# Two of the first block's three up-projection sets as eight plain products, with those on the first heads ahead of the last heads

## Chip, cores, metric

One core of one Trainium2 chip. The metric is the device time of one execution in microseconds; lower is better. Kernels of one batch ran on the same chip beside the kernel before.

## The reference

Linformer attention, then an MLP mixer over tokens and channels:

```python
# batch 8, heads 8, seq 1024, head_dim 64, k_proj 64; d_model 512, d_tok 256, d_ch 1536
k_proj = einsum('ks,bhsd->bhkd', E, k);  v_proj = einsum('ks,bhsd->bhkd', F, v)
attn   = softmax(scale * q @ k_proj^T) @ v_proj
x  = heads side by side                                # (8, 1024, 512)
h  = relu(x^T @ w_tok1) @ w_tok2                       # token mixing
u  = x + h^T
h2 = relu(u @ w_ch1) @ w_ch2                           # "up", then "down"
out = u + h2
```

A block is half a batch: 512 rows of u, 16 blocks in all. Each block has three up-projection sets (`m` = 0, 1, 2).

## The kernel before

Up and down projections use Winograd's variant of Strassen's scheme: seven half-size products in place of eight, paid for with sums on VectorE: sums S of the activations, combinations of the weights (made once, partly in place), and relu-adds on the way out.

```python
def combine(T, b11, b12, b21, b22, cols, name, n, reads):
    def one(k, out, in0, in1, *deps):
        dve(cols, lambda: nc.vector.tensor_sub(out=out, in0=in0, in1=in1), ps=False,
            reads=reads + [(name, n, i) for i in deps], writes=[(name, n, k)])
    one(7, T[1], b22, b12)
    one(5, b12, b12, b11, 7)        # writes over the raw weights b12
    one(6, T[0], b22, b12, 5)
    one(4, T[2], b21, T[0], 6)

def up_set(j, m):                   # seven products of 4 matmuls, 256 columns each
    ...
    product(1)
    act(512, ... copy(view("y"), view("x")) ...)
    product(2);  relu(0, "x")
    product(6);  keep(ub, "ub")
    product(7)
    product(5);  keep(ua, "ua")
    dve(512, ... add_relu(G[:, 2, cs], view("z"), ua) ...)
    product(3);  relu(1, "y")
    product(4)
    dve(512, ... add_relu(G[:, 5, cs], view("z"), ub) ...)
    ... # four totals on VectorE for the down projection
```

The kernel doesn't issue these in the order of the text. Each call of `pe`, `dve`, `act` and so on adds a job with an estimated duration and a priority. A planner then plays the program through when it is built, with a queue for each engine and eight PSUM banks, and takes the job that can start first; among jobs within 0.02 us it takes the one with the lowest priority number:

```python
while any(can.values()):
    pick = None
    for e, js in can.items():
        ...
        t0 = min(c[0] for c in cands) + 0.02
        c = min((c for c in cands if c[0] <= t0), key=lambda c: (c[1], c[2]))
        if pick is None or c[0] < pick[0]:
            pick = c
    ...
return sorted(order, key=lambda j: j.at)
```

What comes out is fixed: each engine runs its instructions in this order.

The softmax here doesn't subtract the row's maximum and nothing guards it: scores larger than these inputs give would overflow.

Of the kernel before, what the change touches and what calls it, by code (L numbers as in the profile page):

```python
# [11 lines left out]
ALU = mybir.AluOpType  # L12
ACT = mybir.ActivationFunctionType
EARLY = 12.0
WHOLE = 3
TWO = 2
SUMS = 60.0
# [181 lines left out]
def kernel(  # L199
# [13 lines left out]
    nc = tc.nc  # L213
    P = 128
# [18 lines left out]
    SETS = CC // 4  # L233
# [20 lines left out]
    def tile_of(shape, dtype, name):  # L254
        return sb.tile(shape, dtype, tag=name, name=name)
# [4 lines left out]
    def bank(b):  # L260

        return banks[b.at] if b.span == 1 else psum[:, b.at : b.at + 2]
# [11 lines left out]
    wc1_sb = tile_of([P, 2, 2, 2, DC // 2], BF16, "wc1_sb")  # L274
# [22 lines left out]
    G_t = [tile_of([P, 7, C2, 2 * P], BF16, f"G{i}") for i in range(2)]  # L297
# [25 lines left out]
    def pe(n, cols, fn, **kw):  # L323
        t = n * MM[cols]
        return pl.add("PE", t, t, fn, **kw)

    def dve(cols, fn, ps=True, **kw):
        t = cols / 960 + 0.07 if ps else cols / 1920 + 0.07
        return pl.add("DVE", t, t + 0.09, fn, **kw)

    def act(cols, fn, **kw):
        t = cols / 1200 + 0.07
        return pl.add("ACT", t, t + 0.105, fn, **kw)
# [40 lines left out]
    for m in range(SETS):  # L374
        cs = slice(m * cw, (m + 1) * cw)
        for ch in range(2):
# [5 lines left out]
                writes=[("w1", m, ch)], prio=next(first),  # L382
            )
    w2_v = moe_w_ch2.rearrange("(ch cc p) d -> p ch cc d", ch=2, p=P)
    for c in range(0, C2, 3):
        for ch in range(2):
            ld(
                0.786, dma(wc2_sb[:, ch, c : c + 3], w2_v[:, ch, c : c + 3]),
                writes=[("w2", ch, c // 3)], prio=next(first),
# [6 lines left out]
    def due_u(s, n):  # L396
        return 8.2 * s + U_AT[n]
# [43 lines left out]
    def combine(T, b11, b12, b21, b22, cols, name, n, reads):  # L441
        def one(k, out, in0, in1, *deps):
            dve(
                cols, lambda: nc.vector.tensor_sub(out=out, in0=in0, in1=in1), ps=False,
                reads=reads + [(name, n, i) for i in deps], writes=[(name, n, k)],
            )

        one(7, T[1], b22, b12)
        one(5, b12, b12, b11, 7)
        one(6, T[0], b22, b12, 5)  # L450
        one(4, T[2], b21, T[0], 6)

    for m in range(SETS):
        cs = slice(m * cw, (m + 1) * cw)
        combine(
            [wT1[:, n, :, cs] for n in range(3)],
            *(wc1_sb[:, dh, :, ch, cs] for dh in range(2) for ch in range(2)),
            cols=2 * cw, name="W1", n=m, reads=[("w1", m, 0), ("w1", m, 1)],
        )
    for c in range(2):  # L460
        cs = slice(3 * c, 3 * c + 3)
        combine(
            [wT2[:, n, cs] for n in range(3)],
            *(wc2_sb[:, ch, cs, dh * DH : (dh + 1) * DH] for ch in range(2) for dh in range(2)),
            cols=3 * DH, name="W2", n=c, reads=[("w2", 0, c), ("w2", 1, c)],
        )
# [46 lines left out]
    def k_transpose_dma():  # L513
        sp(
            2.5,
            lambda: nc.sync.dma_start_transpose(
                out=kT.rearrange("p h c k -> p h (c k)"), in_=kb.rearrange("p h r d -> p (h r d)")
            ),
            reads=[("kb", i, h) for i in range(2) for h in range(H)],
            writes=[("kT", i, h) for i in range(2) for h in range(H)], prio=None,  # L520
        )
# [248 lines left out]
    def quarter(j, sh, dh):  # L770
        return uT_t[j % 2][:, 2 * sh : 2 * sh + 2, 2 * dh : 2 * dh + 2, :]
# [330 lines left out]
    def w1_of(n, dd, c):  # L1102
        cs = slice(c * P, (c + 1) * P)
        if n in (1, 2, 3, 5):
            dh, ch = {1: (0, 0), 2: (1, 0), 3: (1, 1), 5: (0, 1)}[n]
            return wc1_sb[:, dh, dd, ch, cs]
        return wT1[:, {6: 0, 7: 1, 4: 2}[n], dd, cs]
# [7 lines left out]
    def a_of(j, n, dd):  # L1115
        if n in (1, 2, 4):
            sh, dh = {1: (0, 0), 2: (0, 1), 4: (1, 1)}[n]
            return uT_t[j % 2][:, 2 * sh : 2 * sh + 2, 2 * dh + dd, :]
        return S_t[j % 2][:, {5: 0, 6: 1, 7: 2, 3: 3}[n], :, dd, :]
# [4 lines left out]
    def add_relu(out, in0, in1):  # L1124
        nc.vector._custom_dve(TENSOR_ADD_SAT, out=out, in0=in0, in1=in1, s0=FMAX, s1=0.0)  # L1125

    def up_set(j, m):
        s = SETS * j + m
        G = G_t[j % 2]
        cs = slice(2 * m, 2 * m + 2)  # L1130
        bk = {n: Bank("U", seeded=n == "y") for n in "xyz"}
        ub, ua = ub_t[s % 2], ua_t[s % 2]

        def view(n):
            return bank(bk[n]).rearrange("p (c s) -> p c s", c=2)

        def g(n):
            return ("G", j % 2, n, m)

        def mm(n):  # L1140
            t = view(X_OF[n])
            for c in range(2):
                for dd in range(2):
                    nc.tensor.matmul(  # L1144
                        t[:, c, :], w1_of(n, dd, 2 * m + c), a_of(j, n, dd),
                        start=(n in (1, 7) and c == 0 and dd == 0), stop=(c == 1 and dd == 1),
                        skip_group_check=True,
                    )

        def product(n):  # L1150
            src = [("S", j % 2, {5: 0, 6: 1, 7: 2, 3: 3}[n])] if n in (5, 6, 7, 3) else [
                ("uT", j % 2, i) for i in ((0, 1) if n == 1 else (2, 3))
            ]
            src += [("W1", m, n)] if n in (5, 6, 7, 4) else [("w1", m, 0 if n < 3 else 1)]
            first = n in (1, 7)
            b = bk[X_OF[n]]
            pe(
                4, 256, lambda: mm(n), reads=src, takes=[b] if first else [],
                uses=[] if first else [b], prio=due_u(s, n),
                after=[g(i) for i in {1: (0,), 7: (2, 3, 4, 5, 6)}.get(n, ())],  # L1160
            )

        def relu(n, src):
            act(
                512,
                lambda: nc.scalar.activation(out=G[:, n, cs], in_=view(src), func=ACT.Relu),  # L1166
                writes=[g(n)], uses=[bk[src]],
            )

        def keep(dst, name):  # L1170
            act(
                512, lambda: nc.scalar.copy(out=dst, in_=view("y")), writes=[(name, s % 2)],  # L1172
                uses=[bk["y"]],
            )

        def total(n, a, b, add):
            f = nc.vector.tensor_add if add else nc.vector.tensor_sub
            c = slice(2 * both[0], 2 * both[-1] + 2)
            dve(
                512 * len(both), lambda: f(out=G[:, n, c], in0=G[:, a, c], in1=G[:, b, c]), ps=False,  # L1180
                reads=[("G", j % 2, i, mm) for i in (a, b) for mm in both],
                writes=[("G", j % 2, n, mm) for mm in both],
            )

        product(1)
        act(
            512, lambda: nc.scalar.copy(out=view("y"), in_=view("x")), takes=[bk["y"]],  # L1187
            uses=[bk["x"]], after=[g(1)],
        )
        product(2)  # L1190
        relu(0, "x")
        product(6)
        keep(ub, "ub")
        product(7)
        product(5)
        keep(ua, "ua")
        dve(
            512, lambda: add_relu(G[:, 2, cs], view("z"), ua), reads=[("ua", s % 2)],
            writes=[g(2)], uses=[bk["z"]],
        )  # L1200
        product(3)
        relu(1, "y")
        product(4)

        dve(
            512, lambda: add_relu(G[:, 5, cs], view("z"), ub), reads=[("ub", s % 2)],
            writes=[g(5)], uses=[bk["z"]],
        )
        both = TOTALS[m] if SINGLE <= j < NSB - 1 else (m,)
        if both:  # L1210
            total(3, 5, 2, True)
            total(5, 0, 5, False)
            total(4, 3, 0, False)
            total(6, 1, 4, False)

    out_v = out.rearrange("b (p si) d -> b p si d", p=P)

# [191 lines left out]
    def front(b, begin, end):  # L1409
        units = []  # L1410

        def unit(cost, f):
            units.append((cost, f))

        hn = H // 2 if b == 1 else H
        for i in range(H // hn):
# [3 lines left out]
            else:  # L1420
                unit(1.9, lambda t: kv_proj(b, 0, H, t - EARLY, True))
                unit(0.0, lambda t: k_transpose_dma())
# [7 lines left out]
        for h in range(H):  # L1430
            if h + 2 < H:
                unit(0.4, lambda t, h=h: scores(h + 2, t))
            if b >= WHOLE:
                unit(0.5, lambda t, h=h: attend_whole(h, t))
# [46 lines left out]
    for j in plan:  # L1481
# [7 lines left out]
        n = len(nc.cur_bb.bb.instructions)  # L1489
# [37 lines left out]
```

## Time and profile before

| | kernel before |
|---|---|
| time, 3 runs | 423.50 us (422.79 to 423.52) |
| PE busy | 98% of the span |
| VectorE busy | 83%; 100% from 30 to 50 us |
| chain that ended last | PE 91%, VectorE 4%, ScalarE 2%, DMA 1% |

PE (the matrix engine) is the bound. A "hole" below is time between two matmuls beyond their normal spacing (0.109 us at 256 columns). A row of the profile gives 0.27 us for such a matmul, so the rows overlap and short holes do not show in the busy share. The lines, and how they are read, are in the prediction.

### The profile page before, as it was taken

Reading aid. Unit: us, or ns where it says so; the run is one execution under the profiler, and the core shown is the slowest. Engines: PE = TensorE matmul, PEld = TensorE weight load, DVE = VectorE, ACT = ScalarE, POOL = GpSimd, SP = SyncE. Lnnn points to the kernel's source line nnn. Section 1 sums busy time; section 2 is a strip of 40 time slices with the busy share of each in tenths; the row PEclk is TensorE's granted clock in tenths of the full one; section 3 lists DMA queues with packets and bytes.
Section 4 is the critical chain, followed back from the end, with each engine's and each line's share of the span. In section 5 each row is a group of like instructions: output and inputs, shape, how many; then the busy total and the mean of one; then the engine's idle time right before and its main releaser. Section 6 shows DMA issues by size and latency. Waiting matters only on the chain.

```text
span 421.2 us, 9421 instructions
## 1 busy us (share of the span) xinstructions
PE 412.1 (98%) x3838; PEld 347.7 (83%) x3838; DVE 348.0 (83%) x747; ACT 231.8 (55%) x444; POOL 66.2 (16%) x104
## 2 busy tenths in 40 slices
PE   7999999999999999999999999999999999999996
PEld 3587877688788888888798888888898899988885
DVE  2359969679679798988889899898988798997685
ACT  1858884475636546564645556655646645354530
POOL 8453220022003030022103020212100000010110
PEclk9999999999999999999999999999999999999999
DMA  9999999996975989398974989999760501250223
GB/s 166 207 201 206 207 206 164 225 177 140 216 145 103 195 133 235 64 186 141 207 163 94 191 139 224 163 200 179 153 146 0 152 27 76 50 151 2 102 100 103
DMA packets 96668, 62.48 MB, mean 148 GB/s; under 512 B 62064, under 2 KB 92272, under 8 KB 96624
## 3 DMA queue, kind: packets, MB, share of 16 engines
q0 software_dynamic: 34944, 45.09, 54.5%
q1 hardware_dynamic: 61056, 16.00, 21.6%
q10 hardware_dynamic: 624, 0.79, 0.7%
q8 instruction: 30, 0.49, 0.5%
q14 instruction: 14, 0.11, 0.1%
HBM read 59.24 MB, written 16.78 MB: 180 GB/s over the span
## 4 chain that ended last, share of the span: by engine, by line
PE 91%; DVE 4%; ACT 2%; DMA 1%; issue 0%; DVEq 0%
PE psum L1253 34%; PE psum L1144 33%; PE psum L848 4%; PE psum L484 4%; PE psum L597 3%; PE psum L964 3%; PE psum L656 2%; DMA o<-in_F_dram 1%; PE psum L620 1%; DVE u L1071 1%; PE psum L736 1%; PE psum L687 1%; PE psum L581 1%; PE psum L405 1%; PE psum L711 1%; PE psum L1032 1%
## 5 line engine op out<-in xcount | busy, mean ns | idle before, releaser
L1253 PEld LDWEIGHTS <-G 128*128 128x128 bf16 x1344 | 130.6, 98 | 19.7 <-issue 1.5
L1253 PE MATMUL psum<-wc_sb,G 128*128 128x256 bf16 x768 | 102.5, 273 | 0.5 <-ACT psum L1309 0.2
L1166 ACT ACTIVATE G<-psum 128x512 bf16<-128x512 f32 x96 | 57.3, 600 | 56.0 <-PE psum L1144 55.4
L1144 PEld LDWEIGHTS <-wc_sb 128*128 128x128 bf16 x768 | 73.8, 98 | 10.9 <-issue 0.6
L1253 PE MATMUL psum<-wT,G 128*128 128x256 bf16 x576 | 77.7, 273 | 0.1
L1180 DVE TENSOR_TENSOR G<-G 128x512 bf16<-128x512 bf16 (+1 forms) x140 | 69.5, 516 | 1.0
L1144 PEld LDWEIGHTS <-wT 128*128 128x128 bf16 x576 | 55.7, 98 | 9.0 <-issue 1.2
L1144 PE MATMUL psum<-uT,wc_sb 128*128 128x256 bf16 x384 | 57.7, 273 | 0.2 <-ACT psum L1187 0.2
L1144 PE MATMUL psum<-S,wc_sb 128*128 128x256 bf16 x384 | 57.6, 273 | 0.1
L1144 PE MATMUL psum<-S,wT 128*128 128x256 bf16 x384 | 55.6, 273 | 0.4 <-DVE S L781 0.4
L1287 POOL DMA_DIRECT2D out_dram<-o x30 | 16.4, 548 | 240.2 <-DVE o L1293 125.6
L1125 DVE CUSTOM_DVE_ANT_0 G<-psum,ub 128x512 bf16<-128x512 f32 x48 | 32.9, 685 | 15.3 <-PE psum L1144 15.1
L1172 ACT COPY ua<-psum 128x512 f32<-128x512 f32 x48 | 28.2, 588 | 30.1 <-PE psum L1144 29.7
L606 ACT ACTIVATE a<-psum 128x512 bf16<-128x512 f32 x64 | 36.4, 602 | 12.4 <-PE psum L597 11.8
L1293 DVE TENSOR_TENSOR o<-psum,u 128x512 f32<-128x512 f32 x55 | 37.5, 683 | 6.4 <-PE psum L1253 6.3
L1187 ACT COPY psum<-psum 128x512 f32<-128x512 f32 x48 | 27.8, 580 | 18.9 <-DVE G L1125 9.9
L1125 DVE CUSTOM_DVE_ANT_0 G<-psum,ua 128x512 bf16<-128x512 f32 x48 | 32.7, 682 | 5.0 <-ACT ua L1172 4.6
L1172 ACT COPY ub<-psum 128x512 f32<-128x512 f32 x48 | 28.2, 588 | 7.0 <-PE psum L1144 6.3
L1144 PE MATMUL psum<-uT,wT 128*128 128x256 bf16 x192 | 28.8, 273 | 0.1
L673 DVE TENSOR_TENSOR x_sb<-psum,rdn 128x512 bf16<-128x512 f32 x40 | 27.4, 686 | 0.6
L597 PE MATMUL psum<-qT,kT 128*128 128x512 bf16 x64 | 21.5, 380 | 0.6 <-ACT kT L549 0.6
L346 POOL DMA_DIRECT2D v_sb<-in_v_dram x18 | 13.5, 749 | 50.7 <-DMA uT<-u 48.0
(108 smaller groups left out, 547.2 us busy)
## 6 DMA issues: line engine op xcount, KB each, us to landing
out_dram<-o POOLq DMA_DIRECT2D x30, 512.0 KB, 4.2
k_sb<-in_k_dram POOLq DMA_DIRECT2D x14, 512.0 KB, 8.5
v_sb<-in_v_dram POOLq DMA_DIRECT2D x14, 512.0 KB, 10.3
q_sb<-in_q_dram POOLq DMA_DIRECT2D x14, 512.0 KB, 9.9
wc_sb<-in_moe_w_ch_dram POOLq DMA_DIRECT2D x6, 256.0 KB, 12.3
wc_sb<-in_moe_w_ch_dram POOLq DMA_DIRECT2D x4, 384.0 KB, 12.3
k_sb<-in_k_dram POOLq DMA_DIRECT2D x4, 256.0 KB, 6.8
v_sb<-in_v_dram POOLq DMA_DIRECT2D x4, 256.0 KB, 7.3
```

What stands on the lines that cost most here:

```text
L484: nc.tensor.matmul(t[0:KP, 0:hn], ET_sb[:, si, :], k_sb[:, hs, si, :], start=a, stop=z)
L597: lambda: nc.tensor.matmul(bank(bk), kT[:, h].rearrange("p c k -> p (c k)"), qT[:, h].rearrange("p j s -> p (j s)"), start=True, stop=True,),
L606: lambda: nc.scalar.activation(out=a_t[h // 2 % 2][:, h % 2], in_=bank(bk), func=ACT.Exp, scale=scale),
L673: lambda: nc.vector.tensor_tensor(out=x_sb[:, :, h * D : (h + 1) * D].rearrange("p (n c) d -> p n c d", n=2), in0=view()[:, :, :, 0:D], in ...
L1125: nc.vector._custom_dve(TENSOR_ADD_SAT, out=out, in0=in0, in1=in1, s0=FMAX, s1=0.0)
L1144: nc.tensor.matmul(t[:, c, :], w1_of(n, dd, 2 * m + c), a_of(j, n, dd), start=(n in (1, 7) and c == 0 and dd == 0), stop=(c == 1 and dd == 1),
L1166: lambda: nc.scalar.activation(out=G[:, n, cs], in_=view(src), func=ACT.Relu),
L1172: 512, lambda: nc.scalar.copy(out=dst, in_=view("y")), writes=[(name, s % 2)],
L1180: 512 * len(both), lambda: f(out=G[:, n, c], in0=G[:, a, c], in1=G[:, b, c]), ps=False,
L1187: 512, lambda: nc.scalar.copy(out=view("y"), in_=view("x")), takes=[bk["y"]],
L1253: nc.tensor.matmul(to, G[:, G_OF[n], cc, t * P : (t + 1) * P], w2_of(n, cc), start=(n in opens and (t == 0 or alone) and cc == 0), stop=(c ...
L1293: 512, lambda: nc.vector.tensor_add(out=dst, in0=view(src), in1=u_of(sh, dh)),
```

## The change

The intent: before the first product with an S operand, PE waits for VectorE. Plain products need neither S nor combined weights, and those on the first half of the model dimension need only heads 0 to 3. So PE can work while the last heads are finished, at the price of eight groups in place of seven.

```diff
+PLAIN = (0, 1)
@@ combine
+                after=reads if k == 5 else [],
@@
-    for m in range(SETS):
+    def combine_w1(m):
         ...
+    for m in range(SETS):
+        if m not in PLAIN:
+            combine_w1(m)
@@
+    def up_plain(m):
+        ...
+        bk = {(sh, ch): Bank("U") for sh in range(2) for ch in range(2)}
+        quarters = [(0, 0), (0, 1), (1, 1), (1, 0)]
+        for dh in range(2):                       # first heads, then last heads
+            for n, q in enumerate(quarters):
+                pe(
+                    4, 256, lambda q=q, dh=dh: mm(q, dh),
+                    reads=[("uT", 0, 2 * dh + hp) for hp in range(2)] + [("w1", m, q[1])],
+                    takes=[bk[q]] if dh == 0 else [], uses=[bk[q]] if dh else [],
+                    prio=due_u(m, 1) - 1.0 + dh + 0.1 * n,
+                )
+        for q, to in zip(quarters, (0, 1, 2, 5)):
+            act(512, lambda q=q, to=to: nc.scalar.activation(out=G[:, to, cs], in_=view(q), func=ACT.Relu), ...)
+        combine_w1(m)
@@ up_set
+        if j == 0 and m in PLAIN:
+            up_plain(m)
+            both = (m,)
+            totals()
+            return
```

More of the change, by code (lines that the diff above doesn't have):

```diff
@@ L1125, in add_relu, with view, mm @@
         nc.vector._custom_dve(TENSOR_ADD_SAT, out=out, in0=in0, in1=in1, s0=FMAX, s1=0.0)
+    def up_plain(m):
+        G = G_t[0]
+        cs = slice(2 * m, 2 * m + 2)
+        bk = {(sh, ch): Bank("U") for sh in range(2) for ch in range(2)}
+        def view(q):
+            return bank(bk[q]).rearrange("p (c s) -> p c s", c=2)
+        def mm(q, dh):
+            sh, ch = q
+            for c in range(2):
+                for dd in range(2):
+                    nc.tensor.matmul(
+                        view(q)[:, c, :],
+                        wc1_sb[:, dh, dd, ch, (2 * m + c) * P : (2 * m + c + 1) * P],
+                        quarter(0, sh, dh)[:, :, dd, :],
+                        start=(dh == 0 and c == 0 and dd == 0), stop=(c == 1 and dd == 1),
+                        skip_group_check=True,
+                    )
[7 more added lines that the diff above has]
+                    prio=due_u(m, 1) - 1.0 + dh + 0.1 * n,
+                )
+        for q, to in zip(quarters, (0, 1, 2, 5)):
+            act(
+                512,
+                lambda q=q, to=to: nc.scalar.activation(out=G[:, to, cs], in_=view(q), func=ACT.Relu),
+                writes=[("G", 0, to, m)], uses=[bk[q]],
+            )
+        combine_w1(m)
     def up_set(j, m):
@@ L1130, in up_set @@
         cs = slice(2 * m, 2 * m + 2)
-        bk = {n: Bank("U", seeded=n == "y") for n in "xyz"}
+        plain = j == 0 and m in PLAIN
+        bk = {} if plain else {n: Bank("U", seeded=n == "y") for n in "xyz"}
         ub, ua = ub_t[s % 2], ua_t[s % 2]
@@ L1183, in total, with totals @@
             )
+        def totals():
+            total(3, 5, 2, True)
+            total(5, 0, 5, False)
+            total(4, 3, 0, False)
+            total(6, 1, 4, False)
+        if j == 0 and m in PLAIN:
[3 more added lines that the diff above has]
+            return
         product(1)
@@ L1210, in up_set @@
         if both:
-            total(3, 5, 2, True)
-            total(5, 0, 5, False)
-            total(4, 3, 0, False)
-            total(6, 1, 4, False)
+            totals()
     out_v = out.rearrange("b (p si) d -> b p si d", p=P)
```

## The prediction

> **What bounds the kernel now.** I began with the busy shares and the chain that ended last (two parts of the page), then cut the first 100 us into windows, and read the waits, the chain and the timeline only where a window fell short.
>
> ```profile
> PE 412.1 (98%) x3838; PEld 347.7 (83%) x3838; DVE 348.0 (83%) x747; ACT 231.8 (55%) x444; POOL 66.2 (16%) x104
> PE 91%; DVE 4%; ACT 2%; DMA 1%; issue 0%; DVEq 0%
> ```
>
> PE is busy for 98% of the span, and 91% of the chain is PE. The end is set by the time when PE starts to run without a break, plus the PE work that is left then. A saving on another engine counts only where PE waits for it.
>
> PE's own waits are few, and nearly all lie near the start:
>
> ```profile
> PE psum L1085 <- DVE u L1071: 0.5, 1, 0.5
> PE psum L1144 <- DVE S L781: 0.4, 1, 0.4
> ```
>
> In the chain in order of time (start, length, what) the same place is the only long stretch after 28 us that isn't PE:
>
> ```profile
> 28.96 0.40 DVE x_sb L637 x2
> 29.35 0.24 issue
> 29.59 1.28 DVE u L1071 x2
> 30.87 0.33 DVE wT L444
> 31.21 0.60 DVE u L1071
> 31.81 0.33 DVE wc_sb L444
> 32.14 1.20 DVE u L1071 x2
> 33.34 0.15 DVE wT L444
> 33.48 0.10 issue
> 33.59 1.28 DVE u L1071 x2
> 34.87 0.33 DVE wT L444
> 35.20 0.68 DVE S L781 x2
> 35.88 0.04 issue
> 35.93 2.40 PE psum L1144 x20
> ```
>
> From the last attention heads (x_sb) to the first product with an S operand at 35.93 us, VectorE works through residual adds (L1071), the weight combinations of Winograd's scheme for the first set (L444), and the S sums (L781). From 35.93 us on PE runs products. The windows (PE, PEld, DVE, ACT, POOL, clock, DMA share, GB/s) agree:
>
> ```profile
> 30.97:35.93 4.96, 4.06 (x56) 3.48 (x54) 4.96 (x12) 4.66 (x10) 2.90 (x4) 1.00 1.34 203
> 35.93:47.00 11.07, 10.96 (x99) 9.57 (x99) 11.07 (x28) 9.01 (x18) 1.48 (x2) 1.00 1.24 207
> ```
>
> VectorE is full in both; PE has holes only in the first. After 100 us the 20 us windows show 19.7 to 20.0 us of PE, up to the tail. So what the change can win lies almost wholly before 36 us.
>
> **What the skill says, and whether the trace agrees.** (1) "TensorE: Matmul & The Clock Gate", section Back-to-back issue gap, gives a warm matmul of N columns N/2.4 + 2.5 ns, so 109 ns at 256. The timeline agrees: groups of four 256-column products start 0.43 to 0.44 us apart (41.09, 41.52, 41.96), though the rows give 273 ns for one. The row includes the pipeline, so I count 0.109 us and not 0.273. The same page also gives lower sustained figures for other sizes; the trace decides. (2) "VectorE: DVE Perf Modes", section The perf-mode tier table, has tensor_tensor in bf16 from SBUF at twice the rate of one with a PSUM operand. Here the bf16 combination of 512 columns takes 0.33 us and the residual add from PSUM 0.60 to 0.64 us of VectorE (starts in the timeline). It agrees. (3) "Perfetto Trace Analysis", section Identifying the Most-Contended Engine, says matmul busy time is no measure of nearness to the roofline. It applies here: 4.06 us "busy" of 4.96 hides more idle time than 0.9 us, as worked out below.
>
> **The change part by part.**
>
> *Added on PE.* Each of the two sets has eight groups of four matmuls in place of seven: one group more per set, 2 x 4 x 0.109 = **+0.87 us**, and on a full engine it is on the path. Moving data have 256 columns as before, so there is no other cost.
>
> *Filled on PE.* How idle is PE between 30.97 and 35.93 us? The timeline lists 28 transposes (0.056 us apart), 16 matmuls of token mixing with 128 columns (0.058 us) and two groups of products (0.44 us): 1.57 + 0.93 + 0.87 = 3.4 us of work in 4.96, so 1.6 us idle. (Between 28.4 and 30.97 there is no idle time by the same count.) The four plain groups on the first half of the model dimension need only the transposed heads 0 to 3 and the first set's weights. The weights are there in time: PoolE issues the 24th load when a wc_sb load has landed, at 29.3 us, and the next two at 30.9 and 32.2 us; counted down the order of loads, set 0 is complete at about 29 us and set 1 at about 32 us. The transposed heads are copied by ScalarE from 31.45 us, and today's first product starts at 32.33. So plain products can start at 32.0 to 32.3 us: 4 groups of set 0, and one of set 1, since the pool of up-projection banks holds five. That is 5 x 0.44 = 2.2 us of work for a hole of about 1.4 us after 32 us: enough to close it. **-1.3 us**, with 0.1 left for a bank or a late copy.
>
> *Removed from VectorE ahead of the first products.* The four combinations of set 0 (4 x 0.33 = 1.3 us) leave the stretch 30.8 to 35.1, and the plain products do not wait for the S sums. The residual adds of the last heads can then come earlier; that makes sure that the second half of the products (from about 34.3 us) follows without a hole. The time is already in the 1.3 us and isn't counted twice.
>
> *Removed later.* A set loses two relu-adds on VectorE (2 x 0.60 us) and goes from five to four operations on ScalarE. So 2.4 us of VectorE and some 1.1 us of ScalarE fall away between 36 and 55 us. VectorE is full there, but PE scarcely waits: the chain has one place, 38.35 to 40.22, of which PE's timeline shows about 0.27 us of true idle time (the previous group ends near 39.95). This place is in set 0 and goes: **-0.25 us**. The other relief is off the path.
>
> *Moved.* The combinations of sets 0 and 1 come after the plain products that read the raw weights, 8 x 0.33 = 2.7 us, due before the second block's first set. Set 2 and that block's sums come between; from about 34 us VectorE has some 8 us for 4 x 0.33 (set 2's combination) + 8 x 0.33 (two blocks' sums) + 1.2 (set 2's relu-adds) + 4 x 0.33 (set 0's combination) = 6.5 us. It fits, with not much to spare.
>
> Sum: +0.87 - 1.3 - 0.25 = **-0.7 us**, from 423.5 to **422.8 us**.
>
> **The rivals.** (a) *Nothing is won, extra work is paid*: the plain products get no banks while the token-mixing outputs wait in PSUM for VectorE, or take PE ahead of the last heads, whose token mixing and transposes then come late. ScalarE's four copies from 31.45 to 35.3 us, without pause, speak for it: they don't get faster. Then the hole stays and +0.87 is paid: about 424.3 us. Against it: VectorE frees the banks up to 1.3 us sooner. (b) *The combination becomes the new wait*: it writes over weights that plain products read, so it can't run before these end, near 40 us for set 1; VectorE stays at 100% for 15 us. If the second block's first set waits for 1 us, 423.8 us. Against it: the 8 us for 6.5 above, and the planner puts the next batch's attention between. (c) *The static order shifts as a whole.* The order of instructions is planned from estimated durations, and one early change moves banks and priorities everywhere. The present plan has few holes later (0.3 us each at 160 to 180 and 220 to 240 us, some at 80 to 100 and the tail), so there is less to win than to lose: -0.7 to +1 us. (d) *A larger gain*: VectorE's 2.4 us do count, because its queue falls behind the plan by less, and the later holes go as well: about 421.3 us.
>
> **Range and chances.** The arithmetic gives -0.7; its parts alone span about -1.2 (all holes filled) to +0.9 (none). The reshuffled order adds about 1 us either way, and three runs of the kernel before span 0.7 us. That makes 420.8 to 424.4 for 8 in 10. Two per cent is 8.5 us, more than all the PE idle time after the first 10 us, and five times any loss above: faster by over 2% 0.01, within 2% 0.98, slower by over 2% 0.01.
>
> **What would show it right or wrong.** Right: PE starts plain products (a new line, on uT and wc_sb) near 32 us; the waits of PE for VectorE's u and S between 30 and 36 us are gone; PE's work between 32 and 36 us grows by 1.2 us or more; there are 8 more matmuls, and PE's total busy time is about the same while the span is 0.5 to 1 us shorter. Wrong: plain products that start after 34 us, or a wait of PE for L444 or for S between 40 and 45 us (rival b); PE idle time that shows up after 100 us (rival c); or PE work up to 36 us unchanged while the total grows by 0.9 us (rival a).

## The result

| | before | changed |
|---|---|---|
| time, 4 runs each | 423.51 us (422.79 to 424.21) | 424.69 us (424.22 to 425.45) |
| ratio, 95% interval | | 1.003 (1.0005 to 1.0054) |
| span of the profiled run | 421.2 us | 422.3 us |

A ratio here is the mean time of one kernel's fast runs over the mean of the other's fast runs of the same rounds, so it is not quite the ratio of the medians that are quoted.

The kernel got slower by 0.3%: 424.69 us, where 422.8 was forecast with a range up to 424.4. Yet the start went largely as foreseen. First the busy shares and the chain, from the page of the changed kernel:

```profile
PE 413.4 (98%) x3846; PEld 348.4 (83%) x3846; DVE 345.9 (82%) x743; ACT 230.6 (55%) x442; POOL 66.1 (16%) x104
PE 78%; DVE 13%; DMA 4%; ACT 2%; issue 1%; POOL 1%; DVEq 0%; POOLq 0%; ACTq 0%
```

There are eight more matmuls, as foreseen. VectorE's share of the chain went from 4% to 13%, although VectorE has less to do than before (345.9 us, was 348.0). The windows at the start (the same columns as in the prediction):

```profile
30.97:35.93 4.96, 4.71 (x64) 4.37 (x62) 4.48 (x11) 3.21 (x7) 3.00 (x4) 1.00 1.34 203
35.93:47.00 11.07, 10.99 (x104) 9.71 (x102) 11.07 (x31) 9.09 (x18) 1.48 (x2) 1.00 1.24 206
```

From 30.97 to 35.93 us PE now has 4.71 us busy in place of 4.06. The timeline of PE (start, length, line) shows what fills it:

```profile
32.26 0.39 PE L1092 MATMUL psum<-ident,u 128*128 128x128 bf16 x4
32.49 1.91 PE L1147 MATMUL psum<-uT,wc_sb 128*128 128x256 bf16 x16
34.23 0.83 PE L1092 MATMUL psum<-ident,u 128*128 128x128 bf16 x12
35.29 0.66 PE L1066 MATMUL psum<-hT_sb,wt_sb 128*128 128x128 bf16 x8 [0.23 <-ACT uT L1098]
35.79 3.66 PE L1147 MATMUL psum<-uT,wc_sb 128*128 128x256 bf16 x32
```

The plain products are line L1147. Four groups start at 32.49 us, eight follow from 35.79 and the last four at 39.50. There is one short wait, for ScalarE's copy of a transpose. Counted by the spacing of matmuls, PE was idle for 1.39 us between 32 and 36 us in the kernel before and is idle for 0.46 in this one, and the hole of 0.27 us at 39.95 is gone. A new one of 0.23 us stands at 42.57, where a product waits for a ScalarE copy (L1244). It is too short for the list of waits. In the waits of PE over the whole span, those for VectorE's u and S near 35 us are gone:

```profile
PE psum L1307 <- ACT psum L1363: 0.4, 1, 0.4
...
PE psum L1190 <- DVE S L788: 0.3, 1, 0.3
...
PE psum L1066 <- ACT uT L1098: 0.2, 1, 0.2
```

The wait for S that is listed is another one, at 373 us. Where did the time go, then? Late windows, first of the kernel before:

```profile
280.00:340.00 60.00, 60.00 (x561) 52.33 (x559) 52.23 (x108) 33.99 (x64) 4.98 (x8) 1.00 0.56 120
340.00:400.00 60.00, 60.00 (x555) 54.00 (x553) 49.97 (x96) 28.69 (x54) 3.19 (x6) 1.00 0.23 71
```

and of the changed kernel:

```profile
280.00:340.00 60.00, 59.86 (x557) 51.73 (x555) 52.49 (x111) 33.78 (x64) 4.95 (x8) 1.00 0.78 143
340.00:400.00 60.00, 59.66 (x550) 53.55 (x548) 51.12 (x97) 28.98 (x54) 3.20 (x6) 1.00 0.23 71
```

After 280 us, with the change long past, PE gets through 4 and 5 matmuls less in the same time. By the spacing of matmuls its idle time from 280 to 400 us is 1.37 us, and 0.31 in the kernel before. One such place, in the chain in order of time of the changed kernel:

```profile
363.98 0.68 DVE G L1132
364.66 0.60 DVE u L1001
365.26 0.60 DVE a L1001
365.86 0.60 DVE o L1347
...
372.44 0.60 DVE G L1132
373.04 0.68 DVE S L788 x2
373.72 0.04 issue
373.76 0.60 PE psum L1190 x4
```

VectorE works for 10 us on end, and PE waits for the S sums behind it (a hole of 0.42 us). The profile of the kernel before has only PE in its chain there.

**A ledger of PE's idle time.** To put numbers to it I took every matmul of the timeline, gave it its spacing (0.109 us at 256 columns, 0.216 at 512, 0.056 at 128; the projections of k and v, which run side by side (their starts are 0.01 us apart), once a pair), and subtracted the sum from the time passed. This needs a profile with all its matmul records; the five of the table have them. The clock is started 1.2 us after VectorE's first residual add, because the add itself starts at a time that hangs on the landing of the loads (26.9 to 28.3 us in these five), for which a kernel isn't to blame: one load of the token weights is issued at 8.72 or 8.73 us in all fourteen profiles, and lands between 19.8 and 21.1. The last three rows belong to experiments below.

| profile | idle to +23 us | idle from +23 to +380 us | work over before | sum against before | span less start of first add |
|---|---|---|---|---|---|
| before | 2.57 | 3.92 | 0 | 0 | 394.04 |
| changed | 1.37 | 5.23 | 0.87 | +0.98 | 395.00 |
| after_order_from_52 | 1.15 | 4.46 | 0.87 | -0.01 | 393.84 |
| one_set_order_from_56 | 1.43 | 4.46 | 0.44 | -0.16 | 393.74 |
| one_set_order_from_180 | 1.42 | 3.81 | 0.44 | -0.82 | 393.26 |

The changed kernel won 1.20 us of idle time in the first 23 us, paid 0.87 us of work, and was then 0.3 us ahead, about half of what was predicted. Over the next 357 us it collected 1.31 us more of idle time than the kernel before. The last column, which doesn't depend on the count, agrees to 0.2 us.

A sixth profile, that of `one_set_own_order` (below), has all its records too, and closes as well. Counted once more with slightly different spacings, it has 1.23 us less idle time than the kernel before at the start, 2.92 us more later and 0.44 us more work, +2.13 us in all. Its last column is 396.17, also +2.13.

Two cautions. The row of the changed kernel is one profile, of an execution of 424.22 us, its fastest; a second profile of the same kernel (`after_again`) has 396.21 in the last column. And the granted clock in the first 20 us was 0.90 and 0.93 in the changed kernel's profile and 1.00 in the other. The ledger starts behind this: from 20 us on both have 1.00.

### The profile page after: what moved, and what is told of

It reads as the page before. It is cut to its first block, busy times and chain, and to the rows that moved or that the text cites. A ratio compares the mean times of both kernels' runs of the same rounds, so it can differ in the third digit from the quotient of the medians.

```text
span 422.3 us, 9433 instructions
## 1 busy us (share of the span) xinstructions
PE 413.4 (98%) x3846; PEld 348.4 (83%) x3846; DVE 345.9 (82%) x743; ACT 230.6 (55%) x442; POOL 66.1 (16%) x104
## 4 chain that ended last, share of the span: by engine, by line
PE 78%; DVE 13%; DMA 4%; ACT 2%; issue 1%; POOL 1%; DVEq 0%; POOLq 0%; ACTq 0%
PE psum L1307 30%; PE psum L1190 28%; PE psum L855 4%; DMA q_sb<-in_q_dram 3%; PE psum L491 3%; PE psum L971 2%; DVE G L1226 2%; PE psum L604 2%; DVE G L1132 2%; PE psum L663 2%; DMA v_sb<-in_v_dram 2%; DVE u L1007 1%; DVE a L1001 1%; PE psum L1147 1%; DVE o L1347 1%
## 5 line engine op out<-in xcount | busy, mean ns | idle before, releaser
L1212 ACT ACTIVATE G<-psum 128x512 bf16<-128x512 f32 x92 | 54.6, 598 | 59.9 <-PE psum L1190 59.5
L1190 PEld LDWEIGHTS <-wc_sb 128*128 128x128 bf16 x736 | 70.8, 98 | 11.4 <-issue 0.4
L1190 PEld LDWEIGHTS <-wT 128*128 128x128 bf16 x552 | 53.4, 98 | 8.0 <-issue 0.9
L1190 PE MATMUL psum<-uT,wc_sb 128*128 128x256 bf16 x368 | 55.2, 273 | 0.1
L1190 PE MATMUL psum<-S,wc_sb 128*128 128x256 bf16 x368 | 55.1, 273 | 0.0
L1190 PE MATMUL psum<-S,wT 128*128 128x256 bf16 x368 | 53.3, 273 | 0.3 <-DVE S L788 0.3
L1244 ACT COPY psum<-psum 128x512 f32<-128x512 f32 x46 | 26.5, 576 | 23.9 <-PE psum L1190 9.9
L1132 DVE CUSTOM_DVE_ANT_0 G<-psum,ub 128x512 bf16<-128x512 f32 x46 | 31.5, 685 | 9.3 <-PE psum L1190 9.2
L1132 DVE CUSTOM_DVE_ANT_0 G<-psum,ua 128x512 bf16<-128x512 f32 x46 | 31.4, 682 | 8.6 <-ACT ua L1218 8.5
L1218 ACT COPY ub<-psum 128x512 f32<-128x512 f32 x46 | 27.0, 587 | 4.8 <-PE psum L1190 4.0
```

The source lines that it names most:

```text
L1132: nc.vector._custom_dve(TENSOR_ADD_SAT, out=out, in0=in0, in1=in1, s0=FMAX, s1=0.0)
L1190: nc.tensor.matmul(t[:, c, :], w1_of(n, dd, 2 * m + c), a_of(j, n, dd), start=(n in (1, 7) and c == 0 and dd == 0), stop=(c == 1 and dd == 1),
L1212: lambda: nc.scalar.activation(out=G[:, n, cs], in_=view(src), func=ACT.Relu),
L1218: 512, lambda: nc.scalar.copy(out=dst, in_=view("y")), writes=[(name, s % 2)],
L1244: 512, lambda: nc.scalar.copy(out=view("y"), in_=view("x")), takes=[bk["y"]],
```

## The experiments

Theory A: the change does what it should, and the time is lost later, because the planner, given other jobs at the start, orders the whole rest differently, and the new order has more holes. Theory B ("rival B" in the expectations): the change itself costs (extra products, combinations made late, banks), whatever the order.

| label | median us | range us | ratio to before, 95% interval |
|---|---|---|---|
| after_again | 425.04 | 424.22 to 425.48 | 1.0032 (1.001 to 1.0053) |
| after_late_as_before | 424.03 | 423.06 to 424.75 | 1.001 (0.9989 to 1.0031) |
| after_best_order | 425.12 | 422.85 to 425.86 | 1.0031 (1.0006 to 1.0057) |
| before_best_order | 424.84 | 423.36 to 426.62 | 1.003 (1.0003 to 1.0058) |
| before_shaken_1 | 424.62 | 424.48 to 426.98 | 1.0042 (1.0015 to 1.0068) |
| before_shaken_2 | 427.58 | 427.41 to 428.43 | 1.01 (1.008 to 1.012) |
| before_late_as_after | 424.87 | 424.69 to 425.12 | 1.0031 (1.0011 to 1.0051) |
| before_two_more_groups | 424.60 | 423.96 to 425.27 | 1.0025 (1.0005 to 1.0044) |
| after_order_from_52 | 423.36 | 423.10 to 424.11 | 0.999 (0.9974 to 1.0006) |
| one_set_order_from_56 | 422.95 | 422.89 to 423.31 | 0.9985 (0.9971 to 0.9998) |
| one_set_order_from_180 | 422.32 | 422.05 to 422.54 | 0.9967 (0.9954 to 0.9981) |
| one_set_own_order | 425.32 | 425.13 to 426.17 | 1.0041 (1.0026 to 1.0056) |

The kernel before had a median of 423.41 (11 runs) beside the first four, 423.51 (12 runs, those eleven among them) beside the next four, and 423.64 (9 runs) beside the last four. All twelve kernels gave right results.

### The changed kernel again

No edit. It ran on the same chip as the next seven; the last four ran on another.

> The changed kernel once more, to have it on the same chip as the next three. Both theories: 1.0 to 1.5 us (0.3%) slower than the kernel before.

425.04 us: the loss is there again. Its profile shows something else: laid beside the first profile of the same kernel, VectorE's instructions are 0.05 us apart at 57 us, but 0.27 at 107, 0.34 from 110, 0.90 at 126, and that to the end. PE's timeline of the second profile shows two waits that the first doesn't have:

```profile
107.21 0.61 PE L1190 MATMUL psum<-uT,wc_sb 128*128 128x256 bf16 x4 [0.17 <-DMA uT<-u]
125.67 0.39 PE L604 MATMUL psum<-qT,kT 128*128 128x512 bf16 x1 [0.38 <-DMA kT<-kb]
```

Both are for transposing DMAs that SyncE issues. The first took 6.60 us from issue to landing, 5.95 in the first profile, and landed at 107.16 in place of 106.82. The other landed at 125.62 in place of 124.28, as it was issued 2.3 us later. By the spacing of matmuls these two waits are holes of 0.31 and 0.54 us. So this order leaves PE open to the landing of DMAs, which differs between runs of one kernel.

### The changed start, the old order later

The planner gets a list of jobs, `LATE`: those that the kernel before starts after 150 us of planned time, in its order. An engine takes them in just this order, after all its other jobs.

```diff
+LATE = [968, 799, 1171, 830, 636, ...]
+        # lines: each engine's late jobs in order; soon: how many other jobs it has left
+        def may(j):
+            if j.n not in is_late:
+                return True
+            return not soon[j.eng] and lines[j.eng][0] == j.n
@@ the choice of candidates
+                    if not may(j):
+                        continue
@@ once a job is chosen
+            if j.n in is_late:
+                lines[j.eng].pop(0)
+            else:
+                soon[j.eng] -= 1
```

> The changed kernel, in which every engine takes the jobs that the kernel before begins after 150 us of planned time in exactly the order in which the kernel before has them. The plain products and all that precedes stay. Theory A (the start of the change works, 1.25 us of PE idle time filled for 0.87 us of extra products, and the time is lost after 100 us through small holes of another static order): the later holes go, 423.2 to 423.9 us, level with the kernel before and 1 us under the changed kernel; PE's idle time from 150 us to the end as in the kernel before. Rival B (the change itself costs: the extra products, the late weight combinations or the banks slow what follows, whatever the order): stays at 424.5 to 425 us.

424.03 us, 0.1 above the stated band, but 1.0 us less than the changed kernel. The trace makes it sharper. Two instructions of ScalarE's timeline in the kernel before, far apart:

```profile
158.22 0.58 ACT L506 CAST kb<-psum 64x512 bf16<-64x512 f32 x1 [1.39 <-PE psum L487]
...
409.13 0.57 ACT L1309 COPY psum<-psum 128x512 f32<-128x512 f32 x1 [1.85 <-DVE G L1180]
```

and the same two in this kernel:

```profile
158.65 0.58 ACT L600 CAST kb<-psum 64x512 bf16<-64x512 f32 x1 [1.39 <-PE psum L581]
...
409.56 0.57 ACT L1450 COPY psum<-psum 128x512 f32<-128x512 f32 x1 [1.85 <-DVE G L1313]
```

Both are 0.43 us later, and so is every ScalarE instruction sampled between (0.42 or 0.43), down to the same idle time before it. From where the order is the same, the two kernels run the same in these two profiles. So nothing of the change reaches past that point except a fixed distance: theory B can't be right about the stages after it.

### The old start, the changed order later

The mirror image: the kernel before, with the jobs that the changed kernel starts after 100 us of planned time in the changed kernel's order. Same edit, another list.

> The kernel before, without plain products, in which every engine takes the jobs that the changed kernel begins after 100 us of planned time in the changed kernel's order. Theory A: the loss comes with the order, so 424 to 425 us although none of the change is in it. Rival B: 423.2 to 423.8 us.

424.87 us: the loss of the changed kernel, with nothing of the change in it. In the profile every sampled instruction from 104 us on lies 0.73 to 0.78 us behind the same instruction of the changed kernel, to the end. The old start arrives that much later; the seam, time lost where one order goes over into the other, is in this number too.

### Shaking the kernel before

The same work and the same dependencies; priorities are moved at random by at most 0.02 us:

```diff
     def plan(self):
+        rng = random.Random(111)      # 178 in the second
+        for j in self.jobs:
+            if j.prio is not None and j.prio > -100:
+                j.prio += rng.uniform(-0.02, 0.02)
```

Of 240 such draws of the kernel before, the planner's own estimate of PE's end has a median of 417.7 us. Unchanged it is 415.7, which is among the best tenth (run again with seeds 0 to 239, 18 draws are as early or earlier). For the changed kernel the estimate is 418.1, an ordinary value: 240 draws of it have a median of 417.9.

> The kernel before with its jobs' priorities moved by at most 0.02 us at random (planned PE end 418.0 us, the median of the draws, against 415.7 unchanged). Same instructions, same dependencies, another order. Theory A (the order of the kernel before is an unusually good one, and any early change gives it up): 424.0 to 425.5 us, as slow as the changed kernel, with small PE holes after 100 us. Rival B: within 0.3 us of 423.5.

> The same with a poor draw (planned PE end 420.8 us). Theory A: 425 to 428 us, slower than the last. Rival B: within 0.3 us of 423.5.

424.62 and 427.58 us, as theory A has it. A change of no substance costs 1.1 us in the one ordinary draw that was run and 4.1 us in the poor one. The longest PE waits of the second:

```profile
PE psum L1149 <- DVE S L786: 2.0, 2, 1.7
...
PE psum L1149 <- DVE G L1130: 0.9, 1, 0.9
```

Up products wait for VectorE's S sums and relu-adds, which in this order come too late in its queue.

### The best orders by the planner's estimate

1200 draws for each kernel, shaken by up to 0.3 us; the best by planned PE end were run (414.5 us for the changed kernel, 414.65 for the kernel before).

```diff
+        rng = random.Random(203)      # changed kernel, up to 0.2; before: 246, up to 0.3
```

> The changed kernel with its jobs' priorities moved by at most 0.2 us at random, the best of 1200 draws by the planner's own estimate (planned PE end 414.5 us; the changed kernel 418.1, the kernel before 415.7). Theory A: the small holes after 100 us are fewer, so faster than the changed kernel by 1 us or more: 422.3 to 423.3 us. Rival B: 424.5 to 425 us, since the work and the dependencies are the same.

> The kernel before with the best of as many draws (planned PE end 414.65 us; unchanged 415.7), as the fair partner of the last one: Theory A with a change that is worth 0.4 us: 422.5 to 423.3 us, about 0 to 0.5 us over the changed kernel with its best order. Rival B: at 423.5, and 1 us below the changed kernel with its best order.

Both missed: 425.12 and 424.84 us. The first is what rival B expected too; the second is not. The planner's estimate told the one bad order (planned 420.8, measured 427.58) from the middling ones, but these two good ones not. Their runs also spread over 3 us, while the unchanged order mostly keeps to 1.5. The profiles can't say what is lost: matmul records are missing, and the profiled executions are the extremes of their kernels, 422.85 us (the fastest) and 426.62 (the slowest). So the estimate alone did not pick a winner for a whole order.

### The price of the extra work alone

In the kernel before, same order, two groups of the sixth block are computed twice, with the right result:

```diff
-            for c in range(2):
+            for _ in range(2 if n == 1 and j == 5 and m < 2 else 1):
+              for c in range(2):
```

> The kernel before, in the same order, with two product groups of the sixth block computed twice (8 matmuls of 256 columns more, right result), where PE has no holes. The price of the extra work alone: both theories +0.8 to +0.9 us, 424.3 to 424.4 us. If it is much less, PE isn't the bound there and the +0.87 of the prediction was wrong.

424.60 us, 1.0 us up by the means. Laid beside the profile of the kernel before, VectorE's instructions are 0.51 us late ahead of the first doubled group, 0.92 us behind it (at 154 us) and 1.38 us behind the second (at 164 us). That is 0.41 and 0.46 us, 0.87 in all: the +0.87 of the prediction was right, and PE is the bound there. (The first 0.51 is there before any difference between the kernels: the loads landed later in this run.)

### The change in the order of the kernel before

The list of the second experiment, now from 52 us of planned time on, so that only the start is ordered afresh. The shaking can move the free jobs alone; the draw with the least seam was taken.

```diff
+LATE = [...]                          # all that the kernel before starts after 52 us
+        rng = random.Random(3)         # up to 0.3
```

> The changed kernel in which every engine takes all jobs that the kernel before begins after 52 us of planned time in the order of the kernel before; only the 50 us with the plain products are ordered afresh. Theory A (the change is about neutral by itself: 1.25 us of idle time filled for 0.87 us of work, and the loss came with the order): 423.0 to 423.8 us, within 0.3 us of the kernel before; in the trace the distance to the kernel before is fixed by about 60 us and then stays the same to the end. Rival B (the change itself costs 1.4 us): 424.5 to 425 us.

423.36 us against 423.64 for the kernel before; the interval of the ratio includes 1. With the order kept, the change is neutral: the ledger has 1.42 us less idle time by +23 us, 0.87 us more work, and 0.54 us of idle time given back later. The single profiled run, at 422.1 us of span, looks slower than the kernel before's 421.2. VectorE's timeline shows why it isn't. First the kernel before, then this one:

```profile
20.14 0.42 DVE L802 TENSOR_TENSOR wS<-wt_sb 128x512 bf16<-128x512 bf16 x1 [0.68 <-DMA wt_sb<-in_moe_w_tok_dram]
```

```profile
21.14 0.43 DVE L928 TENSOR_TENSOR wS<-wt_sb 128x512 bf16<-128x512 bf16 x1 [1.65 <-DMA wt_sb<-in_moe_w_tok_dram]
```

A load landed 1.0 us later in that run (issued at the same time), and all that follows on it is later. My expectation that the distance is fixed by 60 us was not quite right: from 83 to 91 us it still moves between 0.43 and 0.94 us, and only then stays at 0.92.

### One set in place of two

`PLAIN = (0,)`: half of the extra work. First in the order of the kernel before from 56 us on, then with a free order up to 180 us (best draw, planned end 415.1) and the old order from there, then left to the planner.

```diff
-PLAIN = (0, 1)
+PLAIN = (0,)
+LATE = [...]                          # from 56 us (Random(1)) or from 180 us (Random(7)), shaken by 0.05;
+                                      # neither line in the third kernel
```

> Only the first set plain (half of the extra work, 0.44 us), and the order of the kernel before from 56 us of planned time on. If the first set's four early groups already fill the hole, and the second set's extra group is pure cost: 0.4 us faster than the last kernel and 0.2 to 0.5 us faster than the kernel before, 422.9 to 423.4 us. If the second set is needed to fill the hole: no faster than the last kernel.

> Only the first set plain, an own order up to 180 us of planned time (the best of the draws, planned PE end 415.1 us against 415.7 of the kernel before), from there the order of the kernel before. If the planner's estimate holds here: 0.3 to 0.8 us faster than the kernel before, 422.7 to 423.2 us. The two best draws for a whole order have both missed, so I give this one chance in two; otherwise 423.5 to 424.5 us.

> Only the first set plain, nothing else: the planner orders all afresh (planned PE end 418.2 us, as for the changed kernel with 418.1). Theory A: slower than the kernel before by 0.5 to 2 us, 424 to 425.5 us, although it has half of the extra work and the same idle time filled. Rival B: half of the changed kernel's loss, 424.2 us, and as slow when the order of the kernel before is kept.

422.95 us: 0.41 us under the two-set kernel in the old order, close to the 0.44 us of a group. In the ledger one set has 1.43 us of idle time by +23 us and two sets in the old order 1.15: on this pair the second plain set fills 0.28 us and costs 0.44. (The two starts are different draws, so the 0.28 is rough. With orders left to the planner, my recount finds the same idle time by +23 us with one set as with two, 1.46 us.) Then 422.32 us, better than the band that I gave even odds: 0.33% under the kernel before, with an interval that excludes 1, and the best. Here the planner's estimate did pick well; it is one case against the two misses. Left to the planner the same change takes 425.32 us. Between 422.32 and 425.32 lie 3.0 us with the same work and the same dependencies.

## Why the prediction was wrong

- **PE is the bound; only its holes and its work count.** Right. The ledger closes on PE alone to 0.2 us.
- **+0.87 us for eight more matmuls.** Right: 0.87 measured alone.
- **-1.3 us of idle time filled, from 32.0 to 32.3 us.** The mechanism was right, the size too large: idle time between 32 and 36 us fell by 0.93 us, and so the sign "grows by 1.2 us or more" was missed. Plain products start at 32.49. Only four groups ran early, not five, and PE still waited for a copy by ScalarE (0.38 us by the spacing of matmuls, 0.23 by the rows). The -0.25 of the place at 40 us came as foreseen (0.27). Together the two terms and the rest of the start came to 1.20 us by +23 us, in place of 1.55. One set alone fills most of it (1.14 of 1.42 us in the old order).
- **The late combinations fit (rival b).** Right: no wait of PE for them in the list of waits. The new hole of 0.23 us at 42.57 ends with a ScalarE copy, not with a combination.
- **Plain products without banks or in the way (rival a).** Did not happen: PE's busy time before 35.93 us grew.
- **The order shifts (rival c).** This step failed. The prediction named it, and saw that there was "less to win than to lose", but then entered it into the range as "about 1 us either way", with its middle at zero in the sum. It is not centred on zero. The order of the kernel before is among the best tenth of its own neighbourhood by the planner's estimate, and the chip agrees: all six kernels whose whole order was made afresh (the changed kernel, one set in its own order, two shaken, two best draws) were slower than it, by 1.1 to 4.1 us. A change at the start draws a new order. The term measured +1.31 us in the profile; with the 0.35 us that the start fell short, that is the whole way from the -0.7 of the sum to the +0.98 of the ledger. The means of the first four experiments give the same: the changed kernel 1.4 us over before, 0.4 with the old order after 150 us.
- **A larger gain (rival d).** Did not happen in the changed kernel.

One bound in the prediction was read from busy rows and is too small: it has 8.5 us as more than all the idle time of PE after the first 10 us. By the spacing of matmuls that is about 11 us in the kernel before, 4.1 of them before 28.4 us.

That the constants of the kernel before were chosen with times at hand would explain its good order, but no run shows how they were chosen.

## What to carry to other kernels

If a tuned kernel has its instruction order from a planner, an edit at one place buys a new draw for the whole program. If the old draw was a good one, as here, count that as a loss to be expected, not as noise about zero. To measure the edit itself, keep the old order for all that comes after it; two pairs of programs with the same late order then ran at a fixed distance, to 0.05 us or so, so that one trace beside another shows what an edit is worth where single runs scatter by a microsecond. It isn't certain: two profiles of the changed kernel itself moved 0.85 us apart through late DMAs, so look for a wait on a DMA before you trust a distance. And fill a hole with no more extra work than it takes: the second plain set added 0.44 us, and filled 0.28 on one pair of kernels and nothing on another.

## What the Trainium skill lacked or had wrong

- "TensorE: Matmul & The Clock Gate", section Back-to-back issue gap, calls N/2.4 + 2.5 ns a figure for an isolated matmul and gives 81 ns (128 columns) and 131 ns (512 columns) for a stream of weight loads and matmuls. Here such streams ran at or near the isolated figure: 16 matmuls of 128 columns with weight loads in 0.89 to 1.00 us (0.056 to 0.063 each), 16 of 512 in 3.45 us (0.216 each), in the chain of the kernel before.
- "Perfetto Trace Analysis", section Identifying the Most-Contended Engine, calls the matmul busy share no good measure of nearness to the roofline; it doesn't say that the holes which decide here, 0.1 to 0.6 us each, are found by counting matmuls against their spacing: 6.5 us of idle time in 380 us of the kernel before, where PE's rows leave 1.8.
- No page says how much a fixed instruction order is worth: the same instructions took 423.5 and 427.6 us after priorities moved by 0.02 us.
- No page says how far the landing of a DMA moves between runs, and that this shifts what follows: a load issued at 8.72 or 8.73 us landed at 19.8 to 21.1 us over fourteen profiles, and one transposing DMA took 5.95 and 6.60 us in two profiles of the same kernel.
